# Three heads per turn on ScalarE and VectorE as well as TensorE, in a two-layer decode kernel

## The chip, the cores and the metric

The kernel runs on one core of one Trainium2 chip. A core has five engines with instruction streams of their own: TensorE (PE, with its weight loads shown apart as PEld), VectorE (DVE), ScalarE (ACT), GpSimd (POOL) and SyncE (SP), which here only issues transfers. Sixteen DMA engines move data between the chip's memory and the core's on-chip memory. The metric is the time of one execution on the device, in microseconds (us); less is better.

## The reference

Two identical layers are applied to `x`, two rows (B = 2) of 576 numbers. Each layer is attention for one new token over a long cache, and then a mixer with an MLP. Cut to what matters:

```python
def _A_ref(x, k_cache, v_cache, wq, wo):        # B=2, H=32 heads, 16384 keys, 128 wide
    q = (x @ wq) split into heads
    scores = einsum("bhqd,bhkd->bhqk", q, k_cache) * 128 ** -0.5
    p = softmax(scores)
    return einsum("bhqk,bhkd->bhqd", p, v_cache) joined @ wo
def _B_ref(x, w1, w2, w3, w4):                  # F = 4608
    h = gelu(layernorm(x) @ w1); hs = shifted(h) @ w2; x1 = x + hs
    return x1 + gelu(layernorm(x1) @ w3) @ w4
for _ in range(2):                              # same caches and weights both times
    x = x + _A_ref(layernorm(x), K, V, wq, wo)
    x = x + _B_ref(layernorm(x), w1, w2, w3, w4)
```

With both rows there are 64 pairs of row and head, called heads 0 to 63 here. Each has 4 MB of K and 4 MB of V in bf16, and each layer reads all of it.

## The kernel before, in words

**The store.** One large on-chip buffer, `mem`, holds six slots of 4 MB and three small work tiles (`kt`). A K or V tile of a head fills a slot. `plan_all` writes the order of all transfers and their slots by hand (`tile_order`, `place`, `ring`), and SyncE issues them in that order, in one queue; each waits until the slot, or the half or quarter of it, has been released by its last readers (`used`, `Store.release`, `Store.pump`, L98). A layer's weights pass through slots that are free at its end. Five tiles at the end of layer 0 (`held`: K of heads 61 to 63, V of heads 62 and 63) stay where they are and are not read again for layer 1.

**A head.** Half of its keys go through TensorE: eight chunks of 8 transposes (`transposes`, L1133), each copied out of PSUM by ScalarE (`evacuate`, L1143) and multiplied with q (`scores`, L1153). The other half goes through VectorE: four pairs of a multiply (L1181) and a sum (L1185), against q laid out over all partitions (`q_broadcast`, L1086 to L1098: VectorE makes a diagonal, TensorE spreads it, ScalarE copies it). Then come the maximum (`softmax_max`, with a reduction over partitions on GpSimd, L1203), the exponentials on ScalarE (`softmax_exp`, L1211 to L1219), 128 matmuls with V (`pv`, L1244), and a copy of the result (`keep_o`, L1225). These steps of head s-1 are woven into head s in the order that `attention` writes out.

**The graph.** Every operation is put in a `Graph` with what it reads and writes; `emit` turns the dependences into semaphore waits. Each engine runs its operations in this order. ScalarE, VectorE, GpSimd and SyncE run straight through the program. TensorE alone has a loop: `Graph.loop` and `_turn` fold heads 1 to 60 of layer 0 into 20 turns of three heads, and steps 4 to 60 of layer 1 into 19 turns. Waits inside a loop are on semaphores of TensorE's own, which the end of a turn counts down again. A wait on a transfer cannot stand in the loop: GpSimd waits for the transfer and then signals TensorE (`landed`, a relay). VectorE waits for K transfers directly.

**Between the layers.** Layer 1 takes the heads in the order 62, 63, 61, 60, 0, 1, ..., 59. Heads 62 and 63 are all TensorE's: while layer 0 ends, `ahead` transposes K of both in 32 chunks (L660) and `lay` copies them back in place (L678), and `kept_heads` multiplies them with q (L1165) at layer 1's start. Around this stand the end of a layer's attention (`last_head`), the output projection (`heads_projection`), two norms (`two_norms`), the MLP (`cols_projection`, `groups_projection`) and the next layer's norm and q.

## Time and profile before

| | |
|---|---|
| median of 3 runs | 2567.8 us (2566.64 to 2569.78) |
| profiled execution | 2568.3 us, of which span 2566.6 us |
| read from memory | 1094.21 MB, 426 GB/s over the span |
| VectorE busy | 1873.2 us, 73% of the span |
| TensorE busy | 1631.5 us, 64% |
| ScalarE busy | 1219.3 us, 48% |
| GpSimd busy | 161.1 us, 6% |

Times are counted from the first instruction. "DMA share" is the mean busy share of the 16 DMA engines and can come out slightly above 1. A row of the timeline has its start, its length, the engine, the line and the operation; in brackets stands how long the engine was idle before it and what ended that. "issue" means that the engine waited for nothing that the profile shows. The queue rows called "instruction" are the engines' own code being fetched.

### The profile page before, as it was taken

What the parts mean: (1) busy time and instruction counts of PE and PEld (TensorE: products, weight loads), DVE (VectorE), ACT (ScalarE), POOL (GpSimd) and SP (SyncE); (2) the same over time, 40 slices, a digit from 0 to 9 for tenths busy, and PEclk for the clock granted to TensorE, in tenths of its full rate; (3) what the DMA queues carried; (4) which work ended last, traced back from release to release, by engine and by line L of the source; (5) the groups of instructions that cost most, each with busy time, mean ns of one, the idle gap of its engine ahead of it and who ended that gap; (6) DMA issues with size and microseconds to landing.
All of it is one profiled execution on the core that took longest, in us unless ns stands there. A gap on an engine that the chain in (4) does not pass through costs nothing.

```text
span 2566.6 us, 74123 instructions
## 1 busy us (share of the span) xinstructions
PE 1631.5 (64%) x34584; PEld 1596.3 (62%) x34584; DVE 1873.2 (73%) x1897; ACT 1219.3 (48%) x1832; POOL 161.1 (6%) x154
## 2 busy tenths in 40 slices
PE   4666566666656666665776766666666665666566
PEld 3666566666656665665776766656665665666565
DVE  5877777777777777777619977777677777777773
ACT  3544444544444454444545554444454444445442
POOL 0000000000000000000000000000000000000000
PEclk8555555655555555555565555555555555555555
DMA  9999999999999999999999999999999999999998
GB/s 409 431 432 432 430 431 432 433 432 432 431 432 431 433 432 432 432 432 432 387 396 415 431 431 432 432 432 430 432 431 433 431 433 431 430 433 432 432 430 360
DMA packets 44657, 1095.30 MB, mean 427 GB/s; under 512 B 4890, under 2 KB 6302, under 8 KB 9374
## 3 DMA queue, kind: packets, MB, share of 16 engines
q1 hardware_dynamic: 44574, 1094.23, 99.5%
q8 instruction: 48, 0.79, 0.1%
q14 instruction: 35, 0.29, 0.0%
HBM read 1094.21 MB, written 0.00 MB: 426 GB/s over the span
## 4 chain that ended last, share of the span: by engine, by line
DMA 64%; DVE 28%; PE 6%; issue 2%; ACT 0%; SPq 0%; POOL 0%; another core or an unknown queue 0%; DVEq 0%; POOLq 0%
DMA mem<-in_A_k_cache_dram 61%; DVE s_dve L1185 17%; DVE prod L1181 9%; DMA mem<-in_B_w_dram 2%; PE mps L1244 2%; PE tps L1133 2%; PE sps L1095 1%; PE tps L660 1%; DMA mem<-in_A_wq_dram 0%; PE sps L869 0%; DVE diag L1092 0%; DVE mx L1200 0%; PE sps L801 0%; DVE mx L1197 0%; PE sps L1165 0%
## 5 line engine op out<-in xcount | busy, mean ns | idle before, releaser
L1143 ACT ACTIVATE mem<-tps 128x1024 bf16<-128x1024 bf16 x1008 | 1019.1, 1023 | 868.7 <-PE tps L1133 851.9
L1185 DVE TENSOR_REDUCE s_dve<-prod 128x16 f32<-128x2048 bf16 x504 | 1152.1, 2286 | 17.3
L1133 PE MATMUL tps<-ident,mem 128*128 128x128 bf16 x8064 | 986.5, 300 | 172.1 <-POOLq L177 171.0
L1181 DVE TENSOR_TENSOR prod<-mem,qb 128x2048 bf16<-128x2048 bf16 x504 | 616.5, 1223 | 538.0 <-DMA mem<-in_A_k_cache_dram 520.8
L1244 PE MATMUL mps<-p,mem 128*128 128x1 bf16 x16384 | 514.3, 165 | 592.1 <-ACT p L1219 515.9
L1133 PEld LDWEIGHTS tps<-ident,mem 128*128 128x128 bf16 x8064 | 750.7, 136 | 181.6 <-POOLq L177 180.2
L1244 PEld LDWEIGHTS mps<-p,mem 128*128 128x128 bf16 x16384 | 487.1, 104 | 602.6 <-ACT p L1219 596.8
L1153 PEld LDWEIGHTS sps<-q_col,mem 128*128 128x128 bf16 x8064 | 406.3, 113 | 0.3 <-ACT mem L1143 0.3
L1153 PE MATMUL sps<-q_col,mem 128*128 128x1 bf16 x8064 | 394.0, 170 | 0.1
L1203 POOL PARTITION_ALL_REDUCE mx<-mx x128 | 158.4, 1238 | 2351.8 <-DVE mx L1200 2285.6
L1211 ACT ACTIVATE mx<-mx 128x1 f32<-128x1 f32 x128 | 26.0, 203 | 327.8 <-POOL mx L1203 327.8
L1095 PE MATMUL sps<-diag,ones_bf 128*128 128x128 bf16 x126 | 36.2, 288 | 123.8 <-DVE diag L1092 123.8
L1095 PEld LDWEIGHTS sps<-diag,ones_bf 128*128 128x128 bf16 x126 | 13.2, 105 | 134.1 <-DVE diag L1092 134.1
L1098 ACT ACTIVATE qb<-sps 128x128 bf16<-128x128 f32 x126 | 34.9, 277 | 73.4 <-PE sps L1095 73.2
L1216 ACT ACTIVATE p<-s_dve,mx 128x64 bf16<-128x64 f32 x126 | 43.8, 348 | 4.1
L1197 DVE TENSOR_REDUCE mx<-sps 128x1 f32<-128x64 f32 x128 | 27.6, 215 | 17.8 <-PE sps L1165 12.0
L678 ACT ACTIVATE mem<-tps 128x1024 bf16<-128x1024 bf16 x32 | 30.9, 1022 | 16.5 <-PE tps L660 16.4
L1219 ACT ACTIVATE p<-sps,mx 128x64 bf16<-128x64 f32 x128 | 37.7, 294 | 0.1
L1225 DVE COPY o_acc<-mps 128x1 f32<-128x1 f32 x128 | 19.0, 148 | 18.1 <-PE mps L1244 18.1
L1092 DVE TENSOR_SCALAR diag<-ident,q_f 128x128 bf16<-128x128 bf16 x126 | 30.9, 245 | 0.0
L660 PE MATMUL tps<-ident,mem 128*128 128x128 bf16 x256 | 27.5, 288 | 1.0 <-issue 1.0
L1194 DVE TENSOR_REDUCE mx<-s_dve 128x1 f32<-128x64 f32 x126 | 26.3, 209 | 0.1
(111 smaller groups left out, 286.0 us busy)
## 6 DMA issues: line engine op xcount, KB each, us to landing
mem<-in_A_v_cache_dram SPq DMA_DIRECT2D x126, 4096.0 KB, 49.9
mem<-in_A_k_cache_dram SPq DMA_DIRECT2D x124, 4096.0 KB, 41.2
mem<-in_B_w_dram SPq DMA_DIRECT2D x10, 864.0 KB, 14.8
mem<-in_A_wq_dram SPq DMA_DIRECT2D x8, 1024.0 KB, 12.7
mem<-in_B_w_dram SPq DMA_DIRECT2D x7, 1152.0 KB, 14.5
mem<-in_A_wo_dram SPq DMA_DIRECT2D x6, 1152.0 KB, 37.3
mem<-in_A_k_cache_dram SPq DMA_DIRECT2D x4, 1024.0 KB, 8.9
mem<-in_B_w_dram SPq DMA_DIRECT2D x6, 576.0 KB, 7.2
```

Of the source, the lines that this page charges most:

```text
L660: ins = pe.transpose(self.tps[t][:, j * 128:(j + 1) * 128], buf[:, j * 128:(j + 1) * 128], self.ident[:, :])
L1095: self.pe(lambda pe: pe.matmul(qps, lhsT=self.ones_bf[:, :], rhs=self.diag[:, :], start=True, stop=True, skip_group_check=True), reads=["o ...
L1098: self.act(lambda e: e.activation(out=self.qb[s % 2][:, :], in_=qps, func=ACT.Copy), reads=[("qps", i)], writes=[("qb", s % 2)])
L1133: ins = pe.transpose(self.tps[t][:, j * 128:(j + 1) * 128], buf[:, j * 128:(j + 1) * 128], self.ident[:, :])
L1143: self.act(lambda e: e.activation(out=self.kt[k], in_=self.tps[t][:, :].rearrange("p (i c) -> p i c", i=self.CH), func=ACT.Copy), reads=[( ...
L1153: ins = pe.matmul(self.sps[sp][:, c * self.CH + j:c * self.CH + j + 1], lhsT=self.kt[k][:, j, :], rhs=self.q_col[:, sp:sp + 1], start=True ...
L1181: self.dv(lambda e: e.tensor_tensor(out=prod, in0=buf.rearrange("p (j d) -> p j d", d=128), in1=qbc, op=ALU.mult), reads=[("qb", s % 2)] + ...
L1185: self.dv(lambda e: e.tensor_reduce(out=sd[:, c0:c0 + DB], in_=prod, axis=AX.X, op=ALU.add), reads=["prod"], writes=[("s_dve", s % 2)])
L1203: self.pool(lambda e: e.partition_all_reduce(self.mx[:, 3, m:m + 1], self.mx[:, 2, m:m + 1], channels=128, reduce_op=ROP.max), reads=[("mx ...
L1216: self.act(lambda e: e.activation(out=p[:, n:self.NB], in_=self.s_dve[s % 2][:, 0:self.NB - n], func=ACT.Exp, bias=self.mx[:, 4, m:m + 1], ...
L1219: self.act(lambda e: e.activation(out=p[:, 0:n], in_=self.sps[i][:, 0:n], func=ACT.Exp, bias=self.mx[:, 4, m:m + 1], scale=self.scale, acc ...
L1244: ins = pe.matmul(self.mps[:, 448:449], lhsT=buf[:, j * 128:(j + 1) * 128], rhs=p[:, col:col + 1], start=(h == 0 and b == 0), stop=(h == 1 ...
```

## The change

All three of TensorE, ScalarE and VectorE now run heads 1 to 63 of each layer as 21 turns of three heads. What differs from head to head must be the same instruction in each turn, so:

- columns of `q_f`, `o_acc`, `l1`, `l2` are numbered by the step s and addressed by the turn's register (`Graph.column`); q is copied in the order of the steps (`runs`), and the results are put back in the order of heads (`normed`);
- `qb`, `s_dve` and `mx` have three buffers (two, two and four before);
- every operation has at most one engine that it signals (`to`), with a semaphore for each pair of engines; another engine that waits for such an operation waits for the next operation of the same engine that has no `to` (`_stand_in`);
- VectorE's wait for a K tile goes through GpSimd too, with a relay of its own;
- a step asks for q of the next one (`q_broadcast(s + 1)`) even in the last step, and `keep_o(s - 2)` is there even in the first, where it writes a column that nobody reads;
- layer 1's order is 63, 61, 62, 0, ..., 60. Only head 63 is TensorE's alone: 14 of its 16 chunks are transposed ahead (32 chunks of two heads before), the last two at layer 1's start. Heads 61 and 62 run in the loop like the others. The order of slots (`ring`) changes with it: V of head 61 is the first tile loaded, in four parts, then K of head 0, K of head 1 in two parts, V of head 0, and so on.
- beside it, the selector for the last block of x is made by one more VectorE copy inside the norms (`twice`) and used by one matmul, where two constant matrices and two matmuls were used.

The arithmetic of a head is otherwise the same, and so are the tiles read from memory. The core of the diff:

## Prediction

> **What bounds the kernel now.** The page comes first: the span, the busy shares, and the rows of the DMA engines.

> ```profile
> span 2566.6 us, 74123 instructions
> PE 1631.5 (64%) x34584; PEld 1596.3 (62%) x34584; DVE 1873.2 (73%) x1897; ACT 1219.3 (48%) x1832; POOL 161.1 (6%) x154
> ...
> GB/s 409 431 432 432 430 431 432 433 432 432 431 432 431 433 432 432 432 432 432 387 396 415 431 431 432 432 432 430 432 431 433 431 433 431 430 433 432 432 430 360
> ...
> q1 hardware_dynamic: 44574, 1094.23, 99.5%
> q8 instruction: 48, 0.79, 0.1%
> q14 instruction: 35, 0.29, 0.0%
> ```

> No compute engine is over 73% busy, while the transfers stand at 430 to 433 GB/s in nearly every fortieth of the span. They fall off at three places only: the start, the change of layers (387, 396, 415) and the end (360). 1095 MB at 432 GB/s are 2535 us, so all that is not plain transfer is some 32 us. The second view is the stretches.

> ```profile
> 300.00:900.00 600.00, 376.76 (x7935) 369.21 (x7936) 449.32 (x428) 285.06 (x431) 38.17 (x31) 0.57 1.00 432
> 1270.00:1280.00 10.00, 9.64 (x258) 9.47 (x256) 2.03 (x7) 6.25 (x12) 0.00 (x0) 0.67 0.56 209
> 1290.00:1300.00 10.00, 8.62 (x176) 8.54 (x176) 0.81 (x5) 4.22 (x6) 0.00 (x0) 0.61 0.87 298
> 1300.00:1310.00 10.00, 8.61 (x187) 7.96 (x184) 0.90 (x6) 5.00 (x6) 0.00 (x0) 0.56 1.02 417
> 1310.00:1320.00 10.00, 8.38 (x197) 7.72 (x195) 1.55 (x10) 7.74 (x10) 0.00 (x0) 0.92 1.02 423
> 1320.00:1330.00 10.00, 8.05 (x194) 7.73 (x194) 0.96 (x7) 5.00 (x7) 0.35 (x1) 0.59 1.02 408
> 1370.00:1380.00 10.00, 6.79 (x173) 6.71 (x174) 9.17 (x8) 4.01 (x9) 1.24 (x1) 0.50 0.83 356
> 1380.00:1390.00 10.00, 7.58 (x135) 7.42 (x132) 9.83 (x10) 6.20 (x11) 1.25 (x1) 0.50 1.04 418
> 2530.00:2540.00 10.00, 5.92 (x196) 5.65 (x192) 2.39 (x14) 0.20 (x1) 0.00 (x0) 0.50 1.04 409
> 2540.00:2550.00 10.00, 6.22 (x132) 5.98 (x132) 2.13 (x14) 1.69 (x3) 0.00 (x0) 0.50 1.01 416
> ```

> The last two columns are the DMA share and GB/s. In the steady heads the share is 1.00. Only 1270 to 1280, 1290 to 1300 and 1370 to 1380 show DMA engines without work: at these places compute time is on the path, nowhere else between the start and 2550. The timeline and the DMA issues say how far the steady part is from the edge.

> ```profile
> 640.80 0.33 SPq L98 DMA_DIRECT2D mem<-in_A_k_cache_dram  x1
> ...
> 643.24 0.77 PEld L1133 LDWEIGHTS tps<-ident,mem 128*128 128x128 bf16 x8 [1.51 <-POOLq L177]
> 643.24 1.22 DVE L1181 TENSOR_TENSOR prod<-mem,qb 128x2048 bf16<-128x2048 bf16 x1 [4.52 <-DMA mem<-in_A_k_cache_dram]
> ```

> ```profile
> mem<-in_A_k_cache_dram SPq DMA_DIRECT2D x124, 4096.0 KB, 41.2
> ```

> ```profile
> DVE prod L1181 <- DMA mem<-in_A_k_cache_dram: 520.8, 113, 5.5
> ...
> PE sps L1095 <- DVE diag L1092: 123.8, 126, 8.9
> ```

> A 4 MB tile takes 9.7 us at 432 GB/s, but is issued 41.2 us before it lands, so 31.5 us of other transfers are queued ahead of it. VectorE, the busiest engine, sits idle for 520.8 / 113 = 4.6 us per head, waiting for K. A release that comes late by less than 31 us, or work on VectorE of less than 4.6 us per head, changes nothing there.

> **The change part by part.** *Loops on ScalarE and VectorE.* 21 turns in each layer, each with a branch and a few counts on semaphores. Three heads give VectorE 13.8 us of idle time to hide a turn's end; ScalarE is less busy. TensorE's loop shows what a turn costs it:

> ```profile
> q1 hardware_dynamic: 16142, 470.23, 100.3%
> q14 instruction: 15, 0.12, 0.0%
> q8 instruction: 1, 0.02, 0.0%
> ```

> This is the queue table of 110 to 1200 us. TensorE goes round some 18 times in it, yet q8, which brings 16 KB packets, moves one: its code is fetched once and the turns run from what is held. That q8 is TensorE's follows from the count: 34584 matmuls less 117 looped heads of 257, plus two bodies of 771, are 6057; with as many weight loads, 12114 instructions, and 0.79 MB over them is 65 bytes each. I take a turn at nothing; the bounds are 0 and, if the 4.6 us were gone from every head, whatever it costs in full. [...]

> *Columns by register.* Three operations per head on VectorE, two on ScalarE.

> ```profile
> L1185 DVE TENSOR_REDUCE s_dve<-prod 128x16 f32<-128x2048 bf16 x504 | 1152.1, 2286 | 17.3
> ...
> L1092 DVE TENSOR_SCALAR diag<-ident,q_f 128x128 bf16<-128x128 bf16 x126 | 30.9, 245 | 0.0
> ...
> L660 PE MATMUL tps<-ident,mem 128*128 128x128 bf16 x256 | 27.5, 288 | 1.0 <-issue 1.0
> ```

> The address is not in the trace. Between nothing and as much again as the diagonal (245 ns) three times is 0 to 0.7 us of 4.6 us idle: nothing on the path.

> *Waits through GpSimd, stand-ins.* GpSimd is busy 6%, and TensorE's transposes, which start through it, start at 643.24 like VectorE's multiply, which does not. A stand-in for the last `pv` group of a V tile is a score of the next head, which waits for its K: some 3 us (the 4.5 us idle of VectorE less the rest) against 31 us queued. Nothing.

> *Code no longer fetched.* Outside its loops TensorE had 9 whole heads (2313 matmuls), two kept ones (512) and 256 transposes ahead; now it has 644 (head 0's keys, 112 transposes ahead, 144 early scores and transposes, two last `pv`). 2437 x 2 x 65 bytes = 0.32 MB less. ScalarE and VectorE issue some 27 instructions per head ((1897 + 1832) / 128 = 29, less the layers' own); 120 heads of them less are 0.21 MB. 0.53 MB at 432 GB/s, all on queues that are full: **-1.2 us** (between 0, if packets slip into gaps, and -2.5, the whole 1.08 MB).

> *Layer 0's end.* The 14 remaining chunks of `ahead` are spent where the first 14 were, up to the MLP's first matrix, so 1260 to 1300 keeps its steps. Here the rows are

> ```profile
> 1266.80 0.22 DVE L1197 TENSOR_REDUCE mx<-sps 128x1 f32<-128x64 f32 x1 [2.37 <-PE sps L1153]
> ...
> 1276.41 24.75 SPq L98 DMA_DIRECT2D mem<-in_B_w_dram  x14
> ```

> VectorE waits 2.37 us for TensorE's last scores of head 63, and from there a chain leads to the release of the first `wo` piece, for which the queue runs dry. The new `q_broadcast(64)` puts into TensorE's order a matmul that waits for VectorE's diagonal: 123.8 / 126 = 1.0 us per head, hidden elsewhere, not here. **+1.0 us** (0 to 2). The same at layer 1's end is covered: the DMA share in 2530 to 2550 is 1.01 to 1.04. `twice` is a copy of 128 columns, while VectorE waits for the norm's matmul anyway: nothing, at most 0.25 us.

> *The MLP's second matrix and q, 1300 to 1322.* 13 chunks of transposes (104 x 0.107 us busy = 11 us of TensorE) disappear. The DMA share is 1.02 there, so the time is the transfers' and TensorE only waits longer for them: nothing.

> *Layer 1's start.* Transfers, in time:

> ```profile
> 1316.46 5.49 SPq L98 DMA_DIRECT2D mem<-in_A_k_cache_dram  x4
> ...
> 1321.63 0.22 DVE L828 COPY q_f<-sps 128x64 f32<-128x64 f32 x1 [7.05 <-PE sps L801]
> ...
> 1322.46 2.61 PE L1165 MATMUL sps<-q_col,mem 128*128 128x1 bf16 x91
> ...
> 1325.98 1.13 PE L1165 MATMUL sps<-q_col,mem 128*128 128x1 bf16 x37 [0.90 <-issue]
> ...
> 1327.14 0.33 SPq L98 DMA_DIRECT2D mem<-in_A_v_cache_dram  x1
> ...
> 1379.24 0.33 SPq L98 DMA_DIRECT2D mem<-in_A_k_cache_dram  x1
> ```

> Now the queue runs dry before 1379.24, where a K tile waits for the slot that head 61, begun only after two kept heads, frees: 10 x (1 - 356/432) = **1.8 us**, which go. In their place head 61 starts some 20 us earlier, right after the early scores. Six tiles of 9.7 us lie between the first and the dry spell, so the first (now V of head 61) ends near 1330. The next, K of head 0, needs head 63's slot: 112 early matmuls at 2.61/91 us from 1322.5 (3.2 us), three chunks of transposes (2.6 us) to the stand-in, the scores after them: 1328.4. That is in time by 1.6 us; a stall of TensorE's code as above (0.9 us) fits in. After it each release leads by 5 us or more: the first half of head 61 is through VectorE by 1333 (two pairs of 1.22 + 2.29 us, and the maximum, from 1325) and its slot is wanted at 1340; head 62 ends at 1356, wanted at 1359; then heads at 15 us each run ahead of tiles at 19.4 us. New dry spell 0, bounds 0 and 3 us.

> **Sum.** 2566.6 - 1.2 + 1.0 - 1.8 = 2564.6 us of span; with 1.7 us around it 2566.3. The profiled execution is 0.5 us above the median, so the median to expect is **2565.8 us**. 0.2%, or 5.1 us, is about what a measurement can tell from no change.

> **The rivals.** *Loop exits stall (slower).* Before, the loop is left three heads ahead of a layer's end; now ScalarE, VectorE and TensorE all leave it in the critical chain after head 63 and need code that may not be there.

> ```profile
> PE mps L1244 <- issue: 4.8, 2, 3.0
> ```

> ```profile
> PEld tps L1133 <- POOLq L177: 5.5, 3, 2.5
> ```

> The first is TensorE in 1300 to 1345, on straight code, the second its only kind of wait ahead of transposes in 1200 to 1260. Up to 3.0 us on each of three engines in series is 9 us at layer 0's end, where the queue is dry anyway: 2575; at 1.7 us each it passes 2571 and at 2.4 each it decides. For it: the chain really passes from VectorE over ScalarE to TensorE. Against: TensorE left its loop near 1211, and no wait there is "issue". *Every turn fetches its body again (slower).* [...] As a mechanism here it shows only where a turn's stall passes 13.8 us, over four times the 3.0 us; at 14.5 us it would give 42 x 0.7 = 29 us, 2595. The trace shows a body of 1542 instructions held, and the new ones have 42 operations or so each. *A dry spell at 1330 (no change).* If TensorE stalls 3 us ahead of head 63's release, and head 61's halves follow late, up to 3 us come back: 2569. *The layers' change shortens (faster).* If TensorE's 11 us of transposes in 1300 to 1322 kept the transfers at 417 instead of 432 GB/s, and dry spells at 1290 shrank too, 30 x 0.04 + 1.3 + some 2 us of stalls: 2561. Against: these are short rows, and the share is full.

> **How the numbers follow.** Forecast 0.55; dry spell 0.20; loop exits 0.13, half of it beyond +5.1; turns 0.04; shorter change 0.08, mostly beyond -5.1. So faster 0.08, same 0.76, slower 0.16 with some room for costs of registers. The forecast's own range is 2563 to 2569; the whole range goes from 2562, all of the gain and none of the loss, to 2574, most of three exit stalls.

> **What would show it.** Right: 432 GB/s between 300 and 900 with VectorE idle 3.5 to 4.6 us before K; under 35 packets on q8 and under 15 on q14; no dry spell near 1375; head 63's last maximum 1 us later. Wrong: idle time put down to "issue" behind the last head, a gap in the DMA share near 1330, or VectorE no longer waiting for K.

## The result, and the profile after

The changed kernel takes 2562.2 us (median of 14 executions, 2560.5 to 2563.2), the kernel before 2568.6 us (14 on the same chip, 2566.6 to 2570.3). The ratio is 0.9974, with a 95% interval of 0.9966 to 0.9982. It is 6.5 us faster, where the forecast, 2565.8 for the 2567.8 us then shown, had 2.0: the sign was right and the size was not. The profiled execution took 2561.0 us, of which 2559.2 us are span, 7.4 us less than before.

The page of the changed kernel, the rows that answer to those of before:

```profile
span 2559.2 us, 75096 instructions
...
PE 1629.4 (64%) x34456; PEld 1593.6 (62%) x34456; DVE 1889.5 (74%) x1925; ACT 1214.9 (47%) x1831; POOL 162.2 (6%) x151
...
GB/s 410 428 432 433 431 431 433 431 431 432 433 430 432 433 430 433 432 431 431 411 374 428 433 431 431 433 431 430 433 433 431 431 433 431 431 433 432 430 434 379
...
q1 hardware_dynamic: 44718, 1094.23, 99.7%
q8 instruction: 29, 0.48, 0.1%
q14 instruction: 15, 0.11, 0.0%
```

The steady fortieths move 430 to 434 GB/s, where they moved 430 to 433, so the 7.4 us do not show there. What rose are the two fortieths in which a layer's transfers end, from 387 to 411 and from 360 to 379; the next after the first of them fell (374 for 396). The code queues moved less: 19 packets fewer on q8 and 20 fewer on q14. The stretches (last two columns: DMA share, GB/s):

```profile
300.00:900.00 600.00, 379.60 (x7967) 371.88 (x7967) 452.13 (x430) 288.47 (x434) 38.18 (x31) 0.57 1.00 432
1270.00:1280.00 10.00, 8.74 (x208) 8.64 (x206) 0.91 (x4) 4.08 (x5) 0.00 (x0) 0.52 0.89 325
1280.00:1290.00 10.00, 8.37 (x171) 8.02 (x169) 3.74 (x25) 4.78 (x8) 0.00 (x0) 0.50 0.81 296
1320.00:1330.00 10.00, 7.64 (x137) 7.37 (x135) 9.06 (x11) 5.18 (x6) 1.25 (x1) 0.50 0.75 283
1370.00:1380.00 10.00, 7.35 (x153) 7.18 (x151) 9.83 (x10) 6.97 (x11) 1.25 (x1) 0.67 1.00 431
```

From 300 to 900 the share is 1.00 and the rate 432 GB/s, to the digit what it was. The dry spell of 1370 to 1380 is gone, and a new one stands at 1320 to 1330.

What shows the gain head by head is the time at which each K tile is there, that is, the start of VectorE's first multiply of a head, behind its wait. The same head in both timelines, before and then after:

```profile
388.73 1.23 DVE L1181 TENSOR_TENSOR prod<-mem,qb 128x2048 bf16<-128x2048 bf16 x1 [4.53 <-DMA mem<-in_A_k_cache_dram]
...
409.13 1.22 DVE L1181 TENSOR_TENSOR prod<-mem,qb 128x2048 bf16<-128x2048 bf16 x1 [5.50 <-DMA mem<-in_A_k_cache_dram]
```

```profile
388.76 1.23 DVE L1215 TENSOR_TENSOR prod<-mem,qb 128x2048 bf16<-128x2048 bf16 x1 [4.52 <-POOLq L187]
...
408.20 1.23 DVE L1215 TENSOR_TENSOR prod<-mem,qb 128x2048 bf16<-128x2048 bf16 x1 [4.54 <-POOLq L187]
```

A head takes 19.43 us, 8 MB at 432 GB/s. In the kernel before some heads take 20.40 us: nine times in the two steady stretches K comes late by one step of about 0.97 us, and twice by two halves of it at two heads in a row. In the changed kernel it never does. VectorE's waits from 110 to 1255 us (sum, times, longest) add it up, before and after:

```profile
DVE prod L1181 <- DMA mem<-in_A_k_cache_dram: 274.1, 59, 5.5
```

```profile
DVE prod L1215 <- POOLq L187: 267.3, 59, 4.6
```

As many waits, 6.8 us less, and the longest is 4.6 for 5.5. Cut by landings of K, the span differs like this (us):

| leg | before | after | difference |
|---|---|---|---|
| to K of head 6 of layer 0 | 135.14 | 136.15 | +1.0 |
| from there to K of head 63, layer 0's last | 1114.35 | 1107.47 | -6.9 |
| from there to K of step 11 of layer 1 | 240.65 | 243.98 | +3.3 |
| from there to K of its last step | 1014.20 | 1010.20 | -4.0 |
| to the end of the span | 62.26 | 61.40 | -0.9 |

The whole gain, 10.9 us, lies in the two steady stretches; 3.5 of it are lost elsewhere. The first and the last leg are no finding: the first is 135.1 to 136.2 us in the experiments below without an order that I could see, and a second execution of the changed kernel has 62.61 us for the last.

**Where the step of 0.97 us comes from.** In the kernel before, each of the nine full steps comes some 16 us after an 8-KB packet on q14. The packets' records around the one at 393.0 us (start, duration in ns, queue, bytes) show what it does; the packets of the other chains left out:

```
393.02   325  q14   8192
393.33  1875  q1   32768
395.20  1221  q1   32768
```

The block takes 0.325 us, and the 32-KB packet behind it 1.875 us instead of 1.216: together 0.98 us, the step. The records don't name the engine of a packet. But in the steady part every 32-KB packet starts within 16 ns of another's end, so that the packets join into sixteen chains, one for each DMA engine; where two ends fall within some nanoseconds of each other, two chains may be taken for one another. Worked out in this way from 370 to 1220 us, with the 32-KB packets that each chain moved:

```
kernel before   5 blocks of 0.325 us on one chain (393, 569, 725, 901, 1058)   that chain  695
                5 of 0.309 us on another (441, 618, 796, 975, 1156)            that chain  697
                the other fourteen                                             699 or 700
                besides, two single blocks of 0.309 us (646, 1077)
kernel after    no such trains; two single blocks of 0.309 us (647, 820)       all   699 or 700
```

No chain has a gap in either kernel. So all sixteen engines are always busy, and one of them, which also carries one engine's code, falls four to five packets behind. A tile is there when its last share is (VectorE starts on it 0.55 to 0.71 us later, in a table below), and the 31.5 us of queued transfers let the other fifteen run ahead: the slowest of sixteen sets the pace, while a mean over them in the steady stretch, share or GB/s, hides it (four or five of 11,189 packets). The lag comes out where the queue drains. Ten packets were under way at 1272 us of the kernel before, four at 1274 and one alone at 1276 and 1277, as one engine that is behind would leave it; in the changed kernel there were twelve at 1271, nine at 1273 and sixteen at 1274. Whose code it is, and whether this is the cause, the first two sets of experiments say.

### The profile page after: what moved, and what is told of

Same layout as the page of the kernel before. It is cut to its first block, busy times and chain, and to the rows that moved or that the text cites. A ratio compares the mean times of both kernels' runs of the same rounds, so it can differ in the third digit from the quotient of the medians.

```text
span 2559.2 us, 75096 instructions
## 1 busy us (share of the span) xinstructions
PE 1629.4 (64%) x34456; PEld 1593.6 (62%) x34456; DVE 1889.5 (74%) x1925; ACT 1214.9 (47%) x1831; POOL 162.2 (6%) x151
## 3 DMA queue, kind: packets, MB, share of 16 engines
q1 hardware_dynamic: 44718, 1094.23, 99.7%
## 4 chain that ended last, share of the span: by engine, by line
DMA 66%; DVE 19%; issue 8%; PE 6%; DVEq 0%; ACT 0%; SPq 0%; POOLq 0%; ACTq 0%
DMA mem<-in_A_k_cache_dram 64%; DVE prod L1215 9%; DVE s_dve L1219 8%; PE tps L1158 2%; DMA mem<-in_B_w_dram 2%; PE mps L1272 2%; PE sps L1119 1%; DMA mem<-in_A_wq_dram 0%; PE sps L1184 0%; PE sps L893 0%; DVE diag L1115 0%; DVE mx L1229 0%; PE sps L823 0%; DVE q_col L1109 0%; DVE o_acc L1253 0%
## 5 line engine op out<-in xcount | busy, mean ns | idle before, releaser
L1174 ACT ACTIVATE mem<-tps 128x1024 bf16<-128x1024 bf16 x1018 | 1029.4, 1023 | 848.9 <-PE tps L1158 827.0
L1219 DVE TENSOR_REDUCE s_dve<-prod 128x16 f32<-128x2048 bf16 x508 | 1161.2, 2286 | 17.4
L1158 PEld LDWEIGHTS tps<-ident,mem 128*128 128x128 bf16 x8256 | 770.8, 136 | 160.8 <-POOLq L187 157.0
L1119 PEld LDWEIGHTS sps<-diag,ones_bf 128*128 128x128 bf16 x129 | 13.5, 105 | 124.8 <-DVE diag L1115 124.8
L1115 DVE TENSOR_SCALAR diag<-ident,q_f 128x128 bf16<-128x128 bf16 x129 | 31.5, 244 | 0.0
L823 PE MATMUL sps<-xn,mem 128*128 128x2 bf16 x544 | 21.4, 174 | 9.4 <-DMA mem<-in_A_wq_dram 8.3
L823 PEld LDWEIGHTS sps<-xn,mem 128*128 128x128 bf16 x544 | 20.5, 122 | 10.1 <-DMA mem<-in_A_wq_dram 8.8
L1246 ACT ACTIVATION_READ_ACCUMULATOR p<-sps,mx (+1 forms) x128 | 24.2, 189 | 0.0
## 6 DMA issues: line engine op xcount, KB each, us to landing
mem<-in_A_v_cache_dram SPq DMA_DIRECT2D x125, 4096.0 KB, 47.2
mem<-in_A_k_cache_dram SPq DMA_DIRECT2D x124, 4096.0 KB, 40.9
```

Source lines behind the costliest of these rows:

```text
L823: ins = pe.matmul(out[:, m * B:(m + 1) * B], lhsT=buf[:, c:c + 127 * d + 1:d], rhs=self.xn[:, k, :], start=first and m == lo, stop=False, ...
L1119: self.pe(lambda pe: pe.matmul(qps, lhsT=self.ones_bf[:, :], rhs=self.diag[:, :], start=True, stop=True, skip_group_check=True), reads=["o ...
L1158: ins = pe.transpose(self.tps[t][:, j * 128:(j + 1) * 128], buf[:, j * 128:(j + 1) * 128], self.ident[:, :])
L1174: self.act(lambda e: e.activation(out=self.kt[k], in_=self.tps[t][:, :].rearrange("p (i c) -> p i c", i=self.CH), func=ACT.Copy), reads=[( ...
L1219: self.dv(lambda e: e.tensor_reduce(out=sd[:, c0:c0 + DB], in_=prod, axis=AX.X, op=ALU.add), reads=["prod"], writes=[("s_dve", s % self.NS ...
L1246: self.act(lambda e: e.activation(out=p[:, 0:n], in_=self.sps[i][:, 0:n], func=ACT.Exp, bias=self.mx[:, 4, m:m + 1], scale=self.scale, acc ...
```

## The experiments

### One engine's loop at a time

The changed kernel, with loops on some of the engines only; the others run the same operations as straight code. The edit, here for TensorE and VectorE:

```diff
     def mark(self):
-        return {e: len(self.ops[e]) for e in ("tensor", "scalar", "vector")}
+        return {e: len(self.ops[e]) for e in ("tensor", "vector")}
```

> The changed kernel with ScalarE back on straight code; TensorE and VectorE keep their loops. Theory 1 (code fetches): in the kernel before, K lands 0.97 us late 11 times in the steady heads, and each time a fetch on queue q14 stands just ahead, at a distance of some 8.6 heads; another train of fetches on q14, some 9.1 heads apart, is followed by none. 128 instructions (8 KB) over 14 per head are 9.1 heads, over 15 they are 8.5; VectorE has 14 operations per head and one wait more, so the train that costs is VectorE's and ScalarE's costs nothing: K stays at 19.43 us per head throughout, and the time is that of the changed kernel, 2562 within 2 us. If the costly train is ScalarE's instead: 11 late landings are back, 2562 + 10.7 = 2573. Rival (the gain is from the change of layers): 2562, and no late landing whichever loop is undone.

> The changed kernel with VectorE back on straight code; TensorE and ScalarE keep their loops. Theory 1: the 0.97 us late landings of K are back, some 7 in each layer less those that other delays cover: 2562 + 7 to 13 = 2569 to 2575, with trains of fetches on q14 some 8.6 heads apart. If the costly train is ScalarE's: 2562. Rival (change of layers): 2562 and no late landing.

> The changed kernel with TensorE's loop alone; order of heads, buffers, waits through GpSimd and stand-ins stay. Theory 1: as with VectorE straight, 2569 to 2575, since the two trains of fetches are told apart by which transfers they delay and only one of them does; if both delay the same transfers, up to 2562 + 20 = 2582. Rival (change of layers): 2562.

| loops on | median, us | ratio to before (95%) | slips in layer 0 and 1, us |
|---|---|---|---|
| all three (the change) | 2562.2 | 0.9974 (0.9966 to 0.9982) | 0, 0 |
| TensorE, VectorE | 2564.8 | 0.9988 (0.9979 to 0.9997) | 2.9, 3.0 |
| TensorE, ScalarE | 2571.0 | 1.0012 (1.0003 to 1.0021) | 6.3, 5.8 |
| TensorE | 2571.2 | 1.0012 (1.0003 to 1.0021) | 5.6, 5.8 |
| TensorE in part (before) | 2568.3 (same chip) | 1 | 6.8, 3.8 |

A slip is what an interval between two landings of K has over 19.43 us, summed where it is over 0.2. VectorE's loop alone is worth nearly all of it: against the kernel before on the same chip the times are -6.5, -3.6, +2.7 and +2.9 us, so VectorE's straight code costs 9.2 us, ScalarE's 2.9, and both 9.4. The costs don't add up, and the slips tell why. With VectorE straight (first fence) K is late by some 0.96 us each eighth or ninth head, with ScalarE straight (second) by 0.69 each ninth:

```profile
720.38 1.22 DVE L1215 TENSOR_TENSOR prod<-mem,qb 128x2048 bf16<-128x2048 bf16 x1 [4.54 <-POOLq L187]
740.76 1.22 DVE L1215 TENSOR_TENSOR prod<-mem,qb 128x2048 bf16<-128x2048 bf16 x1 [5.49 <-POOLq L187]
```

```profile
777.52 1.23 DVE L1215 TENSOR_TENSOR prod<-mem,qb 128x2048 bf16<-128x2048 bf16 x1 [4.53 <-POOLq L187]
797.65 1.23 DVE L1215 TENSOR_TENSOR prod<-mem,qb 128x2048 bf16<-128x2048 bf16 x1 [5.23 <-POOLq L187]
```

The trains of blocks sort themselves: at 392, 549, 725, 900 and 1057 when VectorE is straight, at 440, 616, 794, 972 and 1154 when ScalarE is, both when both are, neither with all three in loops. They lie on two different chains. At the 65 bytes an instruction of the prediction's count 8 KB hold an estimated 126, which are 8.4 heads at 15 a head and 9.0 at 14; the blocks of the first train are 166.1 us apart in the kernel before and those of the second 178.6, 8.6 and 9.2 heads of 19.43 us. With both straight, ScalarE's chain is behind too (0.309 us a block and 0.38 us on the packet behind it, 0.69 us), but less than VectorE's, and the slower alone decides. So one half of the expectation failed: ScalarE's train was to cost nothing, and it costs 2.9 us where VectorE's does not hide it.

This can be read without telling the chains apart. In the steady part every engine moves eight packets of 32 KB for each 4-MB tile and then one of 4 bytes (11,189 and 1392 on sixteen chains of the kernel before, from 370 to 1220 us), so the sixteen 4-byte packets of a tile say when each engine's share was done. For the K tile that lands near 1050 us they ended at (us):

| kernel | first fourteen | fifteenth | last | VectorE's first multiply |
|---|---|---|---|---|
| before (both straight) | 1045.49 to 1048.31 | 1050.21 | 1052.71 | 1053.26 |
| loop on TensorE alone (both straight) | 1045.37 to 1048.62 | 1050.26 | 1052.30 | 1052.98 |
| VectorE straight | 1045.38 to 1047.43 | 1048.28 | 1051.90 | 1052.58 |
| ScalarE straight | 1045.20 to 1048.22 | 1048.48 | 1050.26 | 1050.92 |
| all three in loops | 1045.52 to 1047.61 | 1048.57 | 1048.63 | 1049.34 |

Two engines straight leave two DMA engines behind, one leaves one, none leaves none, and VectorE starts 0.55 to 0.71 us after the last of the sixteen.

What the rest of the change is worth is the last two rows of the first table: loops on TensorE alone, with the new order of layer 1 and all else, make the kernel 2.9 us slower, 0.8 of it in slips (11.4 us for 10.6).

### More straight code

If that is so, more code on one engine of the kernel before must cost in proportion, and more on both must cost no more than on the slower one. Four instructions of one column, which change no result, behind each pair of dot products; on VectorE:

```diff
                     self.dots(l, s, u, h, c % n // 2)
+                    for i in range(4 * (c // 2 % 4), 4 * (c // 2 % 4) + 4):
+                        self.dv(lambda e, i=i: e.memset(self.extra[:, i:i + 1], 0.0), writes=[("extra", i)])
```

ScalarE's are copies of a column instead; a third kernel has both.

> The kernel before, with 16 more tiny VectorE instructions in each head (four memsets of 128x1 behind each pair of dot products; they change no result). VectorE's straight code so grows from some 15 to 31 instructions a head, and one 8-KB block lasts 4 heads where it lasted 8 to 9. Theory: every block that VectorE fetches while the transfers are saturated holds up one and the same of the 16 DMA engines by 0.985 us (0.325 us for the block, 0.66 us more for the 32-KB packet behind it), and since each tile needs all 16 engines, K's landings slip by that much. Some 14 blocks in layer 0 and 13 in layer 1 then cost 13 and 12 us where the run before lost 6.6 and 2.95 us: about 2581 to 2585 us, with slips of 0.97 us every fourth head. Rival 1: the fetches are hidden and VectorE's own time counted: 16 instructions of about 0.06 us lie inside the 4.6 us that VectorE idles in a head, so no change, 2568 to 2569 us. Rival 2: the loop gained by its shorter instruction stream alone, whatever is fetched: no change either.

> The kernel before, with 16 more tiny ScalarE instructions in each head (copies of one column). ScalarE's code grows from 14 to 30 instructions a head, one 8-KB block lasts 4 heads instead of 9. Theory (the slowest of 16 engines sets the pace): ScalarE's blocks go to another engine than VectorE's and hold it up 0.69 us each (0.31 us for the block, 0.38 us more for the packet behind it); at today's 6 blocks a layer that engine stays behind VectorE's and costs nothing, at 13 it lags by some 7.5 us at the end of layer 0 and 8 us at the end of layer 1, against 6.6 and 2.95 us measured for VectorE's. So +1 and +5 us, about 2572 to 2575 us, with slips of 0.69 us. Rival: ScalarE's fetches are hidden whatever their number: 2568 to 2569 us. Rival: every fetch adds its time to all others': 13 more of 0.69 us, 2577 to 2578 us.

> The kernel before with both additions, 16 tiny instructions a head on VectorE and 16 on ScalarE. Theory: two engines lag, and only the slower one counts, so the time is that of the kernel with more VectorE instructions alone, within 1 us (about 2581 to 2585 us). Rival (fetches add up wherever they go): that time plus 26 blocks of 0.69 us, 18 us more, about 2600 us.

Against 2567.9 us of the kernel before on the same chip:

| added | median, us | ratio (95%) | slips in layer 0 and 1: count, sum in us |
|---|---|---|---|
| VectorE 16 a head | 2583.8 | 1.0060 (1.0047 to 1.0074) | 14, 13.5; 11, 10.2 |
| ScalarE 16 a head | 2573.3 | 1.0019 (1.0010 to 1.0028) | 12, 7.7; 12, 7.7 |
| both | 2583.3 | 1.0058 (1.0045 to 1.0072) | 14, 13.0; 10, 9.1 |

All three came out inside what the theory gave, and both together cost what VectorE's cost alone. On the page of VectorE's kernel the two fortieths at the layers' ends are 342 and 314 GB/s, for 387 and 360 without the addition, and the steady ones are as they were:

```profile
GB/s 409 429 432 433 431 430 430 431 432 433 430 432 432 430 431 431 433 432 430 342 399 420 430 431 430 433 433 431 430 431 431 432 432 431 432 431 432 431 430 314
```

The rows of VectorE's kernel, a slip between two heads of 19.43 us:

```profile
1000.71 1.22 DVE L1184 TENSOR_TENSOR prod<-mem,qb 128x2048 bf16<-128x2048 bf16 x1 [4.45 <-DMA mem<-in_A_k_cache_dram]
...
1021.11 1.23 DVE L1184 TENSOR_TENSOR prod<-mem,qb 128x2048 bf16<-128x2048 bf16 x1 [5.42 <-DMA mem<-in_A_k_cache_dram]
1040.54 1.22 DVE L1184 TENSOR_TENSOR prod<-mem,qb 128x2048 bf16<-128x2048 bf16 x1 [4.45 <-DMA mem<-in_A_k_cache_dram]
```

and of ScalarE's:

```profile
1035.11 1.23 DVE L1184 TENSOR_TENSOR prod<-mem,qb 128x2048 bf16<-128x2048 bf16 x1 [4.53 <-DMA mem<-in_A_k_cache_dram]
1055.19 1.22 DVE L1184 TENSOR_TENSOR prod<-mem,qb 128x2048 bf16<-128x2048 bf16 x1 [5.18 <-DMA mem<-in_A_k_cache_dram]
```

VectorE still idles 4.45 us in an ordinary head, so its own time isn't what costs; K is late by 0.97 us at each block, four or five heads apart. That the two engines' blocks lie on different DMA engines is worked out from the packets; that costs don't add where they would on one engine is measured (2583.3 us with both, 2583.8 with VectorE's alone).

### The change of layers

The leg between the steady stretches grew by 3.3 us. It takes 241.6 to 242.3 us in the three kernels of the first set, with one loop or two undone, for 244.0 with all three and 240.6 before: some 2 us of the growth appear only with all three loops, and how much of that is due to the DMA engines that are behind in the others was not separated. Three edits of it, with the changed kernel beside two of them once more. The first puts the last chunks of head 63's transposes, which release the slot for K of head 0, ahead of the early scores:

```diff
+            for c in range(2 * n - LEAD, 2 * n):
+                self.transposes(l, 0, o[0], c)
+                pend.append((0, o[0], c, self.chunk))
+                self.chunk += 1
             for h, b, col in self.early:
                 self.early_scores(l, o[0], h * self.BP + b, col)
-            for c in range(2 * n - LEAD, 2 * n):
...
```

> The changed kernel with one thing moved: at layer 1's start the two chunks of head 63 that are transposed late come ahead of the early scores, so that the last reader of its K is an early score, whose release needs no stand-in behind the entry of TensorE's loop. In the changed kernel the transfer of K of head 0 is issued at 1326.81, after a 2.4 us wait of TensorE at the loop's entry, and the transfers stand at 283 GB/s in 1320 to 1330. If the late stand-in is the cause of that dry spell, the issue comes some 3 us earlier, 1320 to 1330 goes up to 350 to 400 GB/s, and the time falls by 2 to 3 us, to 2559 to 2560. If what was loaded first (V of head 61) or its four parts are the cause, it stays at 2562.

It takes 2561.2 us (ratio 0.9972, 0.9961 to 0.9983): not to be told from the change itself. The expectation was half right: the rate at 1320 to 1330 rose to 414 GB/s, but the 2 to 3 us did not come. K of head 0 is issued 3.1 us earlier, but TensorE then enters the loop 2.0 us later, and the next V is issued 1.8 us later. The timeline after, then of this kernel:

```profile
1325.55 0.77 PEld L1158 LDWEIGHTS tps<-ident,mem 128*128 128x128 bf16 x8 [2.63 <-issue]
...
1326.81 12.49 SPq L98 DMA_DIRECT2D mem<-in_A_k_cache_dram  x3
...
1340.89 0.33 SPq L98 DMA_DIRECT2D mem<-in_A_v_cache_dram  x1
```

```profile
1323.70 17.14 SPq L98 DMA_DIRECT2D mem<-in_A_k_cache_dram  x3
...
1327.57 0.77 PEld L1158 LDWEIGHTS tps<-ident,mem 128*128 128x128 bf16 x8 [3.98 <-issue]
...
1342.73 0.33 SPq L98 DMA_DIRECT2D mem<-in_A_v_cache_dram  x1
```

The dry spell moved with it; the stretches of this kernel:

```profile
1320.00:1330.00 10.00, 6.10 (x155) 6.02 (x153) 6.92 (x5) 3.14 (x4) 0.00 (x0) 0.50 1.04 414
...
1340.00:1350.00 10.00, 7.12 (x136) 6.96 (x135) 9.83 (x10) 7.07 (x11) 1.25 (x1) 0.67 0.96 385
1350.00:1360.00 10.00, 9.15 (x207) 9.06 (x204) 9.14 (x9) 4.87 (x6) 0.00 (x0) 0.50 0.91 360
```

The second ends the loops at head 60 and leaves out the q of a 65th head.

```diff
         for s in range(1, U):
+            if s == U - NS:
+                self.g.loop(first, (U - 1) // NS - 1, NS)
...
-                if c == 2 * n - 2:
+                if c == 2 * n - 2 and s < U - 1:
                     self.q_broadcast(s + 1)
...
-        self.g.loop(first, (U - 1) // NS, NS)
```

> The changed kernel with the loops ended one turn earlier (20 turns, heads 1 to 60), heads 61 to 63 written out straight, and the broadcast of the q of a 65th head, which nothing reads, left out. Theory: this broadcast and the 1.36 us that TensorE idles at 'issue' behind the loop's exit made up the 2.7 us that the changed kernel is later at the end of layer 0 than the kernel before; the straight heads make TensorE fetch some nine 16-KB blocks per layer, but its blocks go to different engines (1.5 us each on one engine, so 1.5 us at most for a layer). So between 2558 and 2562 us, 1.4 us earlier at head 63's last maximum. Rival: TensorE's fetches hold one engine, as VectorE's do: nine of 1.5 us in each layer, 2580 us or more. Rival: TensorE runs dry at 'issue' in the straight heads and falls behind: slower than the changed kernel by some us, with issue waits between 1190 and 1250 us.

2562.2 us (0.9978, 0.9969 to 0.9987). Twelve more blocks on q8 (41 for 29) brought one slip of 0.95 us, at the end of layer 1, where six blocks a layer, at some 1.5 us each on one engine, would have cost 9 us each time (the seven blocks of the kernel before between 1384 and 1430 us took 0.93 to 1.06 us, and the packet behind each 1.68 to 1.76 instead of 1.21, together 1.43 to 1.55 us of that engine): these blocks of TensorE's don't hold up one engine. From the last K the last maximum came 0.4 us earlier, not 1.4, and TensorE now stands at "issue" ahead of it; the idle time that I had put to the loop's exit is still there, some 60 us behind it:

```profile
1261.11 0.34 PEld L1273 LDWEIGHTS mps<-p,mem 128*128 128x128 bf16 x10 [0.98 <-issue]
...
1273.86 0.16 PEld L940 LDWEIGHTS sps<-otn,prod 128*128 128x128 bf16 x3 [1.42 <-issue]
```

The third leaves the 65th q where it is, but takes TensorE's wait out of it: VectorE makes the diagonal behind the first pair of dot products. A fourth kernel has this and the first edit (which moves two chunks, not three as its expectation says), and the change itself ran beside them.

```diff
+                if c == 0:
+                    self.q_diag(s + 1)
                 if c == 2 * n - 2:
-                    self.q_broadcast(s + 1)
+                    self.q_spread(s + 1)
...
```

> The changed kernel with VectorE's part of the next head's q (the column and the diagonal) moved from behind the last pair of dot products to behind the first; TensorE's matmul stays where it was and finds the diagonal made. Theory: the broadcast of a 65th q costs the end of layer 0 its 1.35 us (28.27 us from the landing of the last K to the first issue of the MLP's third matrix, 26.92 us in the kernel before) by TensorE's wait for this diagonal, 1.0 us in the mean, so the step falls to about 27.0 us and the time to 2560.5 to 2561.5 us. Rival: the wait is not what makes the step longer, but the new order of layer 1 and the work ahead for it: step 28.3 us, time 2562 us.

> The same, and with the last three chunks of head 63's transposes put ahead of the early scores at layer 1's start. By the theory that the loop's first turn waits at 'issue' for its code wherever the work ahead of it ends, the second edit adds nothing: within 1 us of the first edit alone, 2560 to 2561.5 us. Rival: the two gains add: 1 us more for K of head 0, issued 3 us earlier, 2559 to 2560 us.

> The changed kernel as it is, beside the two edits of it, since they are worth about 1 us each: 2562 us, with 28.3 us from the landing of the last K of layer 0 to the first issue of the MLP's third matrix, and no slip of K's landings.

| kernel | median, us | ratio (95%) | from the last K of layer 0 to the first issue of the MLP's third matrix |
|---|---|---|---|
| change | 2561.8 | 0.9974 (0.9963 to 0.9984) | 1272.19 - 1243.86 = 28.33 |
| diagonal first | 2561.7 | 0.9975 (0.9966 to 0.9984) | 1271.17 - 1243.88 = 27.29 |
| diagonal first, chunks first | 2561.7 | 0.9974 (0.9963 to 0.9985) | 1270.62 - 1243.35 = 27.27 |

The step shortened by 1.04 and 1.06 us as the theory of the wait had it, and the time did not; the second edit added nothing to the first, as expected. The microsecond is gone again by layer 1's steady part. Four kernels are earlier inside this leg, and none arrives at its end by more than half a microsecond earlier (243.5 to 244.6 us for 243.7 to 244.0). What sets that end was not found; that all of them meet the loop's first turn, in which TensorE stands 2.5 to 4 us at "issue", is an argument and no proof. No version beat the changed kernel by a measurable amount.

## Why the prediction was wrong

**Code no longer fetched** is the step that failed: the sum had -1.2 us for it, at most -2.5, and the steady stretches measured -6.9 and -4.0, where all slips are gone. The count of what is no longer fetched was fair (q8 and q14 moved 0.49 MB less, 0.53 was worked out). The price was wrong in kind. It divided bytes by 432 GB/s, the rate of sixteen engines together, which makes an 8-KB block worth 0.02 us. A block of VectorE's goes to one engine and takes 0.98 us of that engine, and each tile waits for the slowest engine: fifty times as much. The 0.32 MB of TensorE's that made up most of the estimate cost little here (twelve of its blocks more brought one slip of 0.95 us), and 0.1 MB of VectorE's nearly all.

**The range** reached the result by luck. With all of the gain and none of the loss the sum's terms give 2566.6 - 2.5 - 1.8 = 2562.3 us of span and, with the 1.2 us that the sum itself adds, 2563.5 us; the lower end of 2562 leaves these 1.2 us out. The rival "the layers' change shortens" came to 2561 and so near to 2562.2, but that leg grew by 3.3 us. "Faster" had a chance of 0.08.

**The view was blind.** "In the steady heads the share is 1.00" is true and does not mean that the engines are even. The trace of before had it in the quoted row of VectorE's waits: 113 waits of 4.6 us, and a longest of 5.5. A wait that ends with a transfer and is now and then one fixed step longer was the sign to follow. The dips at the layers' ends, 387 and 360 GB/s, were read as compute time on the path; a part of them was the slow engine, as the 411 and 379 after the change and the 342 and 314 with more code on VectorE show.

**The bound** was right: the transfers, with 4.6 us idle on VectorE in a head. Loops, columns by register, GpSimd's relays and stand-ins cost nothing there: the wait behind the relay is 4.52 us where the direct wait was 4.53. But work on VectorE of less than 4.6 us a head does not "change nothing": 16 instructions of 0.06 us cost 15.8 us, by their code. The sum took a turn's end at nothing; no run here shows a branch's time, and VectorE's 4.5 us of idle time in a head would hide anything shorter.

**Layer 0's end**, +1.0 us: the step to the MLP's third matrix grew by 28.27 - 26.92 = 1.35 us, of which the diagonal's wait is 1.04, as said. But behind it came 1.36 us of "issue", which the sum lacked and the rival of stalling exits had:

```profile
1274.20 1.15 PEld L893 LDWEIGHTS sps<-oA,mem 128*128 128x128 bf16 x40 [1.36 <-issue]
```

It is one stall of 1.36 us and not three of up to 3.0, and it is not the exit's, as the kernel that leaves the loop a turn earlier has it too. Why it is absent with loops on two engines stays open.

**The MLP's second matrix and q**, nothing: between the third matrix's issue and q's first copy the leg has 1317.13 - 1271.89 = 45.24 us for 1321.63 - 1276.41 = 45.22, with the 1.36 us in it. So some 1.3 us were won there, not nothing.

**Layer 1's start**, -1.8 us and no new dry spell, is the other step that failed: from q's first copy to K of step 11 it came out at 170.47 us for 168.51, +2.0. The old spell is gone as forecast, K of head 0 was issued at 1326.81, earlier than the forecast 1328.4, but the steps ahead of it were earlier still, TensorE stood 2.63 us at the loop's entry where 0.9 had been allowed, and the new spell at 1320 to 1330 is 10 x (1 - 283/432) = 3.4 us. The rival "a dry spell at 1330" (0 to 3 us) was the better account, and two of the prediction's own signs of being wrong are in the trace, the gap near 1330 and the "issue" behind the last head. Why removing the spell did not shorten the leg stays open.

**Every turn fetches its body again** did not happen: the queues of 110 to 1200 us after the change are

```profile
q1 hardware_dynamic: 16147, 470.39, 100.3%
q14 instruction: 3, 0.02, 0.0%
```

three blocks for 15 on q14, and none for one on q8. VectorE's straight code cost 9.2 us, and the branches of its loop nothing that shows. The DMA engines had no free time in which to hide a block: no chain has a gap between 370 and 1220 us.

## What to carry to other kernels

Where transfers bound a kernel, don't take a DMA share of 1.00 and a constant rate for engines that are even: here they were 1.00 and 432 GB/s with nine slips of 0.97 us and without any. Look at the intervals between landings, at the longest wait beside the mean, and at the rate where the queue drains. A stream of code that is fetched while the transfers are saturated can hold up one engine of sixteen, as VectorE's and ScalarE's did here (0.98 and 0.69 us a block), so price it per block as measured and take the slowest engine, not the sum of bytes. A step won at a boundary is worth something only if its end is earlier; compare the landings on both sides before counting it.

## What the runs showed that was not expected

A block of VectorE's code costs the transfers 0.98 us and one of ScalarE's 0.69, both 8 KB: the block itself is alike (0.325 and 0.309 us), the packet behind it is not (1.875 and 1.593 us against 1.216). Each comes back to its own chain each time (five blocks each from 370 to 1220 us of the kernel before), while seven of TensorE's 16-KB blocks between 1384 and 1430 us of the kernel before lay on seven different chains, and took 0.93 to 1.06 us each. What chooses the chain no run shows.
